# Five edits to a gated mix of block attention and a long convolution: where the convolution is added, how one table factor is summed, and a new order

## The chip, the cores and the metric

The kernel runs on one core of one Trainium2 chip. The metric is device time in microseconds of one execution. The engines are named as in the profile: PE (TensorE, the matrix engine; PEld are its weight loads), ACT (ScalarE), DVE (VectorE), POOL (GpSimd) and SP (SyncE, which issues nearly all DMAs here).

## The reference, cut to what matters

```python
x = A_x                                             # (1, 2048, 512) bf16
g = sigmoid((x * gate_w).sum(-1, keepdims=True))    # one gate per token
a = _A_ref(x, wq, wk, wv, wo, beta)                 # 32 heads of 16, 4 segments of 512 tokens
b = _B_ref(x, A_re, A_im, B_re, B_im, C_re, C_im, log_dt, Dskip)
return g * a + (1 - g) * b

# _A_ref, per segment s and head:
#   softmax attention inside the segment, plus a read of a running memory M, z
#   o = sigmoid(beta) * a_mem + (1 - sigmoid(beta)) * a_dot ;  a = concat(o) @ wo
# _B_ref, per channel d:
#   K[d, l] = Re sum_n C[d,n] * exp(dt*A[d,n] * l) * dt*B[d,n]     l = 0 .. 2047 (l rounded to bf16)
#   y = causal convolution of x[:, d] with K[d, :], by FFT ;  b = y + x * Dskip
```

## The kernel before, in words

The program is recorded as some 1,800 operations (class `Sched`). Each has an engine, a function that issues its instructions, and the buffers it reads and writes. The list `ORDER` gives the order of all of them by number, with the buffer slots and, for operations that may run on either engine, whether ACT or DVE takes them. `replay` walks that list; `emit` adds the semaphores. So each engine works through its own queue in a fixed order, and nothing is reordered at run time.

The work falls into these parts, which the order interleaves:

- **Attention.** For each of 4 segments and 4 groups of 8 heads, `project` makes q and k, `scores` makes five score groups. Each group is a matmul in four row tiles into one block of four PSUM banks (banks 0 to 3, the only one for scores), read by one exponential on ACT (L1063, 128x2048, 80 in all). Masks, sums with the values (17 columns a matmul) and normalization follow on PE and DVE. `ophase` reads the memory and transposes the result into `oTT`.
- **Tables.** For each of 4 blocks of 128 channels, `tables` builds powers of exp(dt*A) as two factors, F (20 exponents) and G (32 exponents, multiples of 8). `cmul` makes n new columns of a factor with three DVE products or sums (L1159, L1162, L1166). Then the sums over n of C, B and the powers ("lag") are made on PE: per slice of 4 state rows, four matmuls of 128x64 weights (slices of G) on 40 columns (slices of F), in two column tiles of 64 at `tile_position=(0, 64 * A)`. F and G have one buffer each, so the next block's table begins after these sums.
- **Convolution.** `x_level1` does the first level of a two-level transform of x and parks it in `scr_Z`. `tail` does the rest for two halves of the channels: 16 steps each of x's second level (tag X), K's transform from the tables (tag K), their product on DVE (tag Y), the inverse second level (tag V) and then the inverse first level (tag fir), whose result goes to `scr_C` and is reloaded by token into `CTT`.
- **Output.** `final(s, tb)`, 16 tiles of 128 tokens: on PE, 512 columns of the convolution through the identity, four matmuls of 128 columns that add the skip (x times a diagonal `diagT`), and four of 512 that multiply `oTT` by `wo`; then one scaled read of PSUM on ACT or DVE (L229, L230), and a store.

The gates: `gate_tokens` computes e^z for each token; attention is scaled by e^z (through `oms` and `einvT`) and the final read multiplies everything by 1/(1 + e^z), made for all tokens in `gate_final`.

The token-wise transpose of x comes from PE for segment 0 and from one transposing DMA of 512 KB per segment for the others (L717, issued by SP). All DMAs are issued by SP. The code was recorded with one helper for matmuls, so nearly all PE rows of the profile carry the line of that helper, L683; transposes have lines of their own (L732, L747, L938).

Of the kernel before, what the change touches and what calls it, by code (L numbers as in the profile page):

```python
# [8 lines left out]
BF16 = mybir.dt.bfloat16  # L9
# [339 lines left out]
def c_pe(mode, *ns):  # L349
    return ("P", mode, ns)  # L350
# [16 lines left out]
8/2 22/0 190/0 191 192 194/0 206/1 195 9/4 14/0 0/0 11/1 30/0 10/0 55/1 24/3/1 25v 31/3 26/6/2 6/0 58/2 39/10 40/12 56/4  # L367
1225/0 1243/0/0 1231/3/1 1233/5 27a 1/0 34/13 32/4 33/9 17/0 35 36 37 46/11 15/0 1241/1 38/5 174/0 41/4 179/7 12/0 59v/0
45/13 13/4 47/0 49/1 23/0 57a 201/2/1/1 48 19/0 42 60/3 1244a 62/2 43 44 51/6 61 63v/4 72/2 75v/5 74/6 21/0 73 50/4 54/0
64 202a 84/2 1234a 86/1 18 16 85 87v/2 76 193/0 203 99v/6 52/13 96/2 204/0/0 1242a 589/0 98/2 378/0 97 100 53 28/4/0  # L370
211/7 29a 175/2 108/3 109/1 65 101 205a 294/5/0/2 110 176/0 122/5 77 123v/3 295a 209/1 111v/0 3/0 1232a 180/0 197/4
251/2/2/0 1246/1 213/3 215/0/0/1 120/2 121 88 252a 256/2/1/0 177/1 210a 1245/0 89 212a 1235 182/2 590/1 198/0 178 135v/8
257 591 220/0/1 800/0 221 132/1 66/3 134/6 136 199/0 990v/0 253 258 214v 67/2 133 207/1 222 989v 144/3 137 68 254/2/1
216 112 113 259 208v 2/0 218 145/1 146 5/0 993v/0 159v/7 158/3 997 992v 241/0/3 255a 998/0 242 160 991v 200/0 999
1257/2/1 994 243 1259/1 1260a 80/0 1258a 229/0/2 230 124 78/1 338/1/2 156/3 1247/2/0 1249/3 231 995/1 157 224/0/0 1003
225 339a 379/1 217 161 1261 996 1007/0 1004/1 147v/9 1005 79 219/0/0 380 1000 1248a 223/1 1001/1 1006 125 801/2 1250a
148 1226/3/1 1002 802 226 168v/1 1010/1 237/0/1 238 90/1 1009 91/5 227 1228/2 1008 1227a 239 1251 228 297/3/0 298a 382/0
1011 169 272/0/0 592 170 273 92 296 1262/3/0 1012 232 233/1 1229a 1230 149 236/2 240 244 245 1015 274 1263a 234 263/0/2
264 246/0 260 1013/1 247 102/1 1264/3 235/1 265 1016/0 104/6 1265a 248 103 114/1 267/0/1 268 1266 381 266/1 1014 261/0
1252/2/1 1017 1254/3 1021 269 1236/0/0 115/7 280/0/2 281 1255a 270 271 1238/3 275 1018 1253a 282 116 1019/0 126/1 1020  # L380
1024 276/4 277 1237a 1028/1 1027 249/2 250a/0 278/1 1267/1 1029 284/0/3 285 286 335/0/1/0 593 1025/0 803 987/0 336a
308/0/1 1256 309 279/0 1026 1239a 283 287 1283/1/1 1031/1 1285/2 310 1030 4/0 1286a 288 289/2 304/0/3 1284a 1022/0 305
384/1/2/1 290 1032 340/2/1/1 306 385a 1023 321/0/2 322 1287 341 1037/1/0 1041/3 1038 128/1 1039 1042 127 342 1033/2 323
140/3 1034 1035 313/0/0 1040a 1043a 343 291 314 183 307/1 311 312 386 1050v/0 1036a 315 1052v/0 1049v 1288/0 1048v 1056
196 1057/1 1051v 1275/2/1 1058 117v/4 337 138/1 1240 1062 1046/0 69v/6 1063/1 1273/3 1274a 1276a 325/0/3 326 327 316
1054/0 1289/2/0 317/0 1053 1064 387/3/0 388a 1055 347/0/1 318 1069/1 348 395/0/0 1059 1290a 319/0 1065 299/1/0/0 1066/0
139 349 1067 1074 320/2 324 1277 1045 328 1075/0 300 1291/3 356/0/2 70 129v/5 1292a 329 302 152/4 330/1 331 392 357 396a
1299/0/1 1301/3 81v/7 358 130 1068 1076 301 105v/0 1300a 150/3 1302a 332 351/0/3 352 399/0 292/3 444/1/1 353 93v/3 82
1293 445a 368/0/0 151 1060/0 1077 369 1280/1/0 1070 350/2 354 400a 355 1303 293a 359 1268/0/1 131 370 1278/3 1281a 1279a
106 364/0/1 165v/2 1078/1 1079 365 366 1061 1071 1269a 1270/3 1271a 71 1086 393/1 83 406/0/3 407 1282 1087/0 363/0 367  # L390
1044 166 1088 1272 408 360/3 448/0 361 1072/1 362/1 1296/2/0 394a 333/3 1073 94 334a 95 371 372 373/4 410/0/0 167 411
1047 1080 1090/0 1297a 1294/1 1089 153v/8 397/2 141v/1 374 412 423/0/2 1091 375 154 424 1081/0 1304/3/1 398a 303/0 344
1295a 107 409/1 1306/2 118 1083 425 1298 427/0/3 428 1307a 1305a 1308 164/5 413 1322/0 1084/1 376/2 441/3/1/0 429 345
442a 415/0/1 1085 119 1082 155 416 1100/3/0 1101 1092/0 1093 377a 1094 1309/1 262 443 1096/2 1097 1098 414 391/1 142
162/2 163 383/0 181 417 346 171v/9 1107v/0 1099a 1310/0 1311/2 473/0/0 474 1111v/0 1110v 1113/0 1109v 1108v 1115 422/2
426 418 1116/1 1095a 1102a 1112 419/0 1114 1324/0 1117 542/3/2 420 430 431 1323/1 475 1105 1104 543a 1325/0/2 1326a 1118
# [129 lines left out]
def build_graph(nc, es, A_x, A_wq, A_wk, A_wv, A_wo, A_beta, B_A_re, B_A_im, B_B_re, B_B_im,  # L526
# [12 lines left out]
    def cload(arr, name, dt, key=0.0):  # L539
# [6 lines left out]
        S.dma(lambda: ap(T, n=n), lambda: h[:], 128 * n * sz, w=[T], key=key, q=LQ)  # L546
        return T
# [876 lines left out]
```

## Time and profile before

| | |
|---|---|
| Runs | 314.17, 313.51, 311.81 us; median 313.51 |
| Profiled execution | span 311.6 us from its first to its last instruction; its own time is not given apart from that |
| Granted PE clock, mean | 0.965 |
| First exponential | starts at 26.89 us |
| Last exponential | starts at 283.80 us |
| Last read of an output tile | starts at 305.20 us |
| DMA | 49.94 MB, mean 160 GB/s |

The page gives the busy time of each engine as a share of the span, and the same in 40 slices of 7.8 us, one digit of tenths each. Windows give the same for a chosen stretch. The chain of waits goes back from the last instruction, at each step to what released it. Rows of a timeline give start and duration in microseconds, then engine, line, operation, output and input, shape and count; matmuls that follow each other are merged into one row under the shape of the first. Since matmuls are pipelined, the start of one and the start of the next tell more than their durations.

### The profile page before, as it was taken

Reading aid. Unit: us, or ns where it says so; the run is one execution under the profiler, and the core shown is the slowest. Engines: PE = TensorE matmul, PEld = TensorE weight load, DVE = VectorE, ACT = ScalarE, POOL = GpSimd, SP = SyncE. Lnnn points to the kernel's source line nnn. Section 1 sums busy time; section 2 is a strip of 40 time slices with the busy share of each in tenths; the row PEclk is TensorE's granted clock in tenths of the full one; section 3 lists DMA queues with packets and bytes.
Section 4 is the critical chain, followed back from the end, with each engine's and each line's share of the span. In section 5 each row is a group of like instructions: output and inputs, shape, how many; then the busy total and the mean of one; then the engine's idle time right before and its main releaser. Section 6 shows DMA issues by size and latency. Waiting matters only on the chain.

```text
span 311.6 us, 9347 instructions
## 1 busy us (share of the span) xinstructions
PE 267.4 (86%) x3868; PEld 175.6 (56%) x3868; DVE 262.9 (84%) x638; ACT 270.0 (87%) x323; POOL 3.2 (1%) x9
## 2 busy tenths in 40 slices
PE   1787687698778899899988999999999999879991
PEld 1442354364444666586765576767767667555550
DVE  1999899989999989998999998989994999883440
ACT  2898998999999999989999989999899999985221
POOL 2000000000000000000000000000000000000000
PEclk9997995989998999999999999999999999998999
DMA  5999423151333754656665578787688784466141
GB/s 138 237 230 207 106 87 107 40 143 41 95 91 88 202 142 116 176 166 181 176 189 152 172 202 253 218 238 209 197 251 240 209 253 113 131 177 201 50 135 52
DMA packets 62362, 49.94 MB, mean 160 GB/s; under 512 B 23920, under 2 KB 57712, under 8 KB 62320
## 3 DMA queue, kind: packets, MB, share of 16 engines
q1 hardware_dynamic: 62320, 49.35, 56.7%
q8 instruction: 30, 0.49, 0.7%
q14 instruction: 12, 0.10, 0.1%
HBM read 29.02 MB, written 8.39 MB: 120 GB/s over the span
## 4 chain that ended last, share of the span: by engine, by line
PE 41%; ACT 35%; DVE 9%; DMA 7%; issue 4%; SPq 3%; DVEq 0%; ACTq 0%
PE psum L683 40%; ACT sb L1063 20%; ACT sb L226 12%; SPq L222 3%; DMA sb<-sb 2%; DVE sb L227 1%; DMA sb<-scr_Z 1%; DMA scr_C<-sb 1%; ACT sb L799 1%; DMA sb<-c_ident 1%; ACT sb L941 1%; DVE sb L1271 1%; ACT sb L992 1%; DMA sb<-c_negm 1%; DVE sb L1162 1%
## 5 line engine op out<-in xcount | busy, mean ns | idle before, releaser
L683 PE MATMUL psum<-sb 128*128 128x17 bf16 (+11 forms) x3780 | 261.2, 235 | 30.2 <-ACT sb L1063 17.6
L683 PEld LDWEIGHTS psum<-sb 128*128 128x128 bf16 (+3 forms) x3780 | 168.8, 99 | 119.3 <-ACT sb L1063 33.9
L1063 ACT ACTIVATE sb<-psum 128x2048 bf16<-128x2048 f32 x80 | 152.1, 1901 | 6.6 <-PE psum L683 6.4
L226 ACT ACTIVATE sb<-psum 128x512 bf16<-128x512 f32 (+3 forms) x171 | 100.3, 647 | 7.2 <-PE psum L683 6.4
L227 DVE CAST sb<-psum 128x512 bf16<-128x512 f32 (+1 forms) x52 | 35.3, 692 | 11.7 <-PE psum L683 10.0
L1159 DVE TENSOR_TENSOR sb<-sb 128x512 bf16<-128x512 bf16 (+3 forms) x52 | 34.0, 659 | 0.1
L1166 DVE TENSOR_TENSOR sb<-sb 128x512 bf16<-128x512 bf16 (+3 forms) x52 | 33.8, 661 | 0.1
L1162 DVE TENSOR_TENSOR sb<-sb 128x512 bf16<-128x512 bf16 (+3 forms) x52 | 33.7, 659 | 0.1
L1271 DVE TENSOR_TENSOR sb<-sb 128x1024 bf16<-128x1024 bf16 x32 | 21.8, 682 | 2.4 <-ACT sb L226 1.3
L1075 DVE TENSOR_TENSOR sb<-sb 128x1024 bf16<-128x1024 bf16 (+1 forms) x40 | 22.7, 576 | 1.0 <-ACT sb L1063 0.9
L229 ACT ACTIVATE sb<-psum,sb 128x512 bf16<-128x512 f32 x8 | 5.4, 686 | 14.9 <-PE psum L683 14.9
L1038 DVE TENSOR_TENSOR sb<-psum,sb 128x256 bf16<-128x256 f32 x32 | 13.3, 418 | 0.3
L230 DVE TENSOR_SCALAR sb<-psum,sb 128x512 bf16<-128x512 f32 x8 | 5.9, 747 | 6.9 <-PE psum L683 6.9
L1035 DVE RECIPROCAL sb<-psum 128x16 f32<-128x16 f32 x32 | 8.0, 251 | 4.2 <-PE psum L683 4.2
L799 ACT ACTIVATE sb<-sb 128x512 f32<-128x512 f32 x18 | 11.3, 643 | 0.0
L1115 DVE TENSOR_TENSOR sb<-psum,sb 128x512 bf16<-128x512 f32 x12 | 8.3, 688 | 0.2
L800 DVE TENSOR_TENSOR sb<-sb 128x256 f32<-128x256 f32 x18 | 7.5, 419 | 1.1 <-ACT sb L799 1.1
L747 PE MATMUL psum<-sb 128*128 128x128 bf16 x24 | 2.7, 280 | 6.4 <-DMA sb<-c_ident 6.3
L808 DVE CAST sb<-sb 128x512 bf16<-128x512 f32 x20 | 8.2, 420 | 0.0
L992 ACT ACTIVATE sb<-sb 128x512 bf16<-128x512 bf16 x12 | 7.6, 631 | 0.0
L801 DVE SCALAR_TENSOR_TENSOR sb<-sb 128x256 f32<-128x256 f32 x18 | 7.5, 419 | 0.0
L941 ACT ACTIVATE sb<-psum 128x512 bf16<-128x512 bf16 x12 | 7.3, 609 | 0.2 <-PE psum L938 0.2
(61 smaller groups left out, 92.4 us busy)
## 6 DMA issues: line engine op xcount, KB each, us to landing
sb<-c_DNM SPq DMA_DIRECT2D x32, 320.0 KB, 3.8
sb<-c_DNM SPq DMA_DIRECT2D x32, 192.0 KB, 3.0
sb<-sb SPq DMA_DIRECT2D x84, 64.0 KB, 2.9
scr_Z<-sb SPq DMA_DIRECT2D x16, 256.0 KB, 2.3
sb<-scr_Z SPq DMA_DIRECT2D x32, 128.0 KB, 3.3
sb<-sb SPq DMA_DIRECT2D x32, 128.0 KB
sb<-in_A_x_dram SPq DMA_DIRECT2D x5, 512.0 KB, 4.5
scr_C<-sb SPq DMA_DIRECT2D x8, 256.0 KB, 3.4
```

Of the source, the lines that this page charges most:

```text
L226: fa = lambda e: e.activation(dst(), src(), ACT.Copy)
L227: fd = lambda e: e.tensor_copy(dst(), src())
L683: mm = lambda e, o_, l, r_, st, sp, **kw: e.matmul(o_, lhsT=l, rhs=r_, start=st, stop=sp, skip_group_check=True, **kw)
L799: op("ACT", ("As", 512), lambda e, sq=sq, Z=Z: e.activation(ap(sq, n=512), ap(Z, n=512), ACT.Square), r=[Z], w=[sq], key=PW[h] + PWS * k)
L992: op("ACT", ("Asx", 512), lambda e: e.activation(ap(eq, n=512), ap(qT, n=512), ACT.Exp), r=[qT], w=[eq])
L1038: op("DVE", ("V1", 256), lambda e: e.tensor_tensor(ap(o1, gi * 16, [[128, 4], [32, 4], [1, 16]]), ap(T, dims=[[68, 4], [17, 4], [1, 16]]), ...
L1063: o = op("ACT", ("Ax", 2048), lambda e, P=P, pT=pT: e.activation(ap(pT, n=2048), ap(P, n=2048), ACT.Exp, scale=0.25), r=[P], w=[pT])
L1075: op("DVE", ("V2", 128 * nb), lambda e, pT=pT, dims=dims: e.tensor_tensor(ap(pT, dims=dims + [[1, 128]]), ap(pT, dims=dims + [[1, 128]]), ...
L1159: op("DVE", ("V2" if n > 1 else "V1", 256 * n), lambda e: e.tensor_tensor(run(tile, ne, dst, 1), run(tile, ne, src, sstep), ap(pw, cl * 51 ...
L1162: op("DVE", ("V2" if n > 1 else "V1", 256 * n), lambda e: e.tensor_tensor(run(t2, n, 0, 1), run(tile, ne, src, sstep), ap(pw, cl * 512 + 2 ...
L1166: op("DVE", ("V2" if n > 1 else "V1", 256 * n), lambda e: e.tensor_tensor(D_(), D_(), ap(t2, n * 128, [[-n * 128, 2], [2 * n, 64], [1, 2 * ...
L1271: op("DVE", ("V2", 1024), lambda e, Y=Y, XAB=XAB, K3=K3: e.tensor_tensor(ap(Y, dims=[[512, 2], [1, 512]]), ap(XAB, dims=[[512, 2], [1, 512 ...
```

## The change

1. **Final tiles.** The identity matmul and the skip leave PE. The sum in PSUM is now attention alone, scaled already by g = 1/(1 + e^-z), and DVE adds the convolution times (1 - g) while it reads PSUM, in one operation per tile (L1348). ACT no longer reads final tiles.
2. **Gates.** `gate_tokens` makes e^-z, 1 + e^-z, g and 1 - g per segment, `gate_final` is gone, and one exponential less is made for segments 1 to 3.
3. **Skip.** x times the diagonal is added in the inverse first level: four matmuls of 128 columns in each of 16 groups, with columns of x that are 16 tokens apart as weights.
4. **Table factor G.** Its upper 16 exponents are no longer completed as complex products. One DVE product makes the part that stays in place, two more make the second term, and the sums get the second term as extra matmuls: for each slice four of 128x32 weights, in column tiles of 32 at `(0, 64 * A + 32)`, on top of the four of 128x64.
5. **Loads.** The identity and the first block of x are issued by ACT; the rest by SP as before. Each transposing load is split in four.
6. **Order.** `ORDER` is new throughout. In it some operations change between ACT and DVE, the mask table is loaded earlier, exponentials and sines at the start stand in another order, and fewer of the final tiles stand behind the last exponential.

```diff
-ident = cload(np.eye(128), "ident", BF16, -1)
+ident = cload(np.eye(128), "ident", BF16, -1, q="ACT")
...
 def do_xT(s):
     if s > 0:
-        op("SP", ("D", 524288), lambda e: e.dma_start_transpose(
-            ap(xTT[0], s * 512, dims=[[2048, 4], [1, 512]]), ... [[512, 512], [1, 512]])),
-           w=[xTT[s]], isdma=True, tr=True)
+        for k in range(4):
+            op("SP", ("D", 131072), lambda e, k=k: e.dma_start_transpose(
+                ap(xTT[0], k * 2048 + s * 512, n=512), ... [[512, 512], [1, 128]])),
+               pw=[xTT[s]], isdma=True, tr=True)
...
 # gate_tokens
-    op("ACT", ..., activation(g(expT), g(gzT), ACT.Exp))
-    if s > 0:
-        op("ACT", ..., activation(g(einvT), g(gzT), ACT.Exp, scale=-1.0))
+    op("ACT", ..., activation(g(expT), g(gzT), ACT.Exp, scale=-1.0))
+    op("DVE", ..., tensor_scalar_add(g(einvT), g(expT), 1.0))
+    op("DVE", ..., reciprocal(g(gzT), g(einvT)))
+    op("DVE", ..., tensor_tensor(g(omgT), g(expT), g(gzT), ALU.mult))
...
 # tables
-        gm(16, 0, 1, 8, 7)
-        gm(24, 8, 1, 8, 7)
+        pw = pws[(7, h)]
+        rd = parts(gp, G, 0, 16)
+        op("DVE", ("V2", 4096), tensor_tensor(G[16:32], G[0:16], pw, ALU.mult))
+        tw = [Tile(t2P, BF16) for _ in range(2)]
+        for cc in range(2):
+            op("DVE", ("V2", 2048), tensor_tensor(tw[cc], G half cc [0:16], pw, ALU.mult))
...
                         for cc in range(2):
                             for A in range(2):
                                 pr = 32 * A + sl
                                 i = mm(e, ap(P, ..., p0=64 * A, np_=64), ap(G, (1 - cc) * GPL + pr * 2 * NG, n=2 * NG),
-                                       ap(F, ...), cc == 0, cc == 1, tile_position=(0, 64 * A))
+                                       ap(F, ...), cc == 0, False, tile_position=(0, 64 * A))
+                        for cc in range(2):
+                            for A in range(2):
+                                pr = 32 * A + sl
+                                i = mm(e, ap(P, ..., p0=64 * A + 32, np_=32), ap(tw[cc], pr * 32, n=32),
+                                       ap(F, ...), False, cc == 1, tile_position=(0, 64 * A + 32))
...
 # tail, inverse first level
+                    for j in range(2):
+                        for kk in range(2):
+                            k = 2 * half + kk
+                            i = mm(e, ap(P, j * 256 + kk * 128, n=128), ap(xTT[0], k * 2048 + b0 + j, [[16, 128]]),
+                                   ap(diagT, k * 128, n=128), False, j == 1 and kk == 1)
...
 # final
-            mm(e, ap(P, n=512), ap(ident, n=128), ap(CTT[s], tb * 512, n=512), True, False)
-            for k in range(4):
-                i = mm(e, ap(P, k * 128, n=128), ap(xTT[0], k * 2048 + t0, n=128), ap(diagT, k * 128, n=128), False, False)
-            for hg in range(3 if s == 3 else 4):
+            for hg in range(nh):
                 i = att(e, hg, hg == 3)
...
-        S.evac(lambda: ap(ou, n=512), lambda: ap(P, n=512), 512, r=[P, omgT], w=[ou], scale=lambda: ap(omgT, 4 * s + tb, n=1))
+        op("DVE", ("V1", 512), lambda e: e.scalar_tensor_tensor(ap(ou, n=512), ap(CTT[s], tb * 512, n=512), ap(omgT, 4 * s + tb, n=1),
+                                                                ap(P, n=512), ALU.mult, ALU.add), ...)
```

Two places of the new order matter below. The first is PE's queue around the table sums of the first channel block (64x40 and 32x40 are the outputs of those sums, 128x17 the sums with the values, 128x256 and 128x2x128 a score group and its mask). Before:

```order
L683 MATMUL psum<-sb 128x512 x4
L938 MATMUL psum<-sb 128x128 x4
L683 MATMUL psum<-sb 128x512 x4
L683 MATMUL psum<-sb 128x128 x4
L683 MATMUL psum<-sb 64x40 x128
L683 MATMUL psum<-sb 128x256 x8
L683 MATMUL psum<-sb 128x2x128 x4
L683 MATMUL psum<-sb 128x17 x32
```

and now, where its twelfth slice ends and the thirteenth begins:

```order
L686 MATMUL psum<-sb 64x40 x4
L686 MATMUL psum<-sb 32x40 x4
L686 MATMUL psum<-sb 128x512 x4
L686 MATMUL psum<-sb 128x128 x4
L686 MATMUL psum<-sb 64x40 x4
L686 MATMUL psum<-sb 32x40 x4
```

One run of 128 equal matmuls became 32 pairs of rows, one for each slice, alternating between the two tile shapes, with a score group between the twelfth and the thirteenth; the sums of the second block are cut twice by score groups, those of the third and fourth once by convolution steps or sums with the values.

The second place is the end of PE's queue, the final tiles behind the last score groups. Before, near the last transpose of an attention result:

```order
L683 MATMUL psum<-sb 128x512 x4
L683 MATMUL psum<-sb 128x128 x8
L683 MATMUL psum<-sb 128x512
L683 MATMUL psum<-sb 128x128 x4
L683 MATMUL psum<-sb 128x512 x5
```

and now:

```order
L686 MATMUL psum<-sb 128x512 x4
L686 MATMUL psum<-sb 128x17 x16
L686 MATMUL psum<-sb 128x512 x8
L686 MATMUL psum<-sb 128x128 x8
L686 MATMUL psum<-sb 128x512 x32
```

The identity matmuls (one of each five) and the skip (128x128 x4) are gone from it; the 128x128 rows that are left are the last transpose of an attention result. On DVE the queue now ends with eleven combinations of L1348, where the 16 reads were shared before, eight on DVE (L230) and eight on ACT (L229).

More of the change, by code (lines that the diff above doesn't have):

```diff
@@ L452 @@
[L452 to L455 removed]
+209/0 9/0 8/1 0/0 24/4/0 14/0 1229/0 6/0 1235/0/0 55/1 30/0 1245/1/1 25v 31/0 39/1 40/2 1237/4 3/0 34/3 32/4 1246a
@@ L537, in const, with cload @@
         return nc.inline_tensor(np.ascontiguousarray(arr, dtype=np.float32), name=name)
-    def cload(arr, name, dt, key=0.0):
+    def cload(arr, name, dt, key=0.0, q=LQ):
         arr = np.asarray(arr, np.float32).reshape(128, -1)
@@ L572, in build_graph @@
     omgT = S.keep(64, F32)
+    omgP = [omgT.part() for _ in range(4)]
     gzT = S.keep(64, F32)
@@ L723, in do_xT @@
               lambda: bass.AP(x.tensor, x.offset + s * 4 * 128 * 512, [[512, 128], [128 * 512, 4], [1, 512]]),
-              524288, w=[xks], key=(-0.95 if s == 0 else S.key - 8))
+              524288, w=[xks], key=-0.95, q="ACT")
         S.tag = "xT%d" % s
```

224 lines of the change are left out of this document (117 added, 107 removed).

## The prediction

> **What bounds the kernel now.** I read the page first, then busy time by windows, then the chain that ended last, and last the single rows around the places that the change touches.
>
> ```profile
> PE 267.4 (86%) x3868; PEld 175.6 (56%) x3868; DVE 262.9 (84%) x638; ACT 270.0 (87%) x323; POOL 3.2 (1%) x9
> PE   1787687698778899899988999999999999879991
> DVE  1999899989999989998999998989994999883440
> ACT  2898998999999999989999989999899999985221
> PE 41%; ACT 35%; DVE 9%; DMA 7%; issue 4%; SPq 3%; DVEq 0%; ACTq 0%
> L1063 ACT ACTIVATE sb<-psum 128x2048 bf16<-128x2048 f32 x80 | 152.1, 1901 | 6.6 <-PE psum L683 6.4
> ```
>
> Three engines are near 86%, so the average says little; the windows say more (columns: stretch, length, then busy time and count for PE, PEld, DVE, ACT, POOL, then granted clock, DMA share, GB/s).
>
> ```profile
> 60.00:80.00 20.00, 16.34 (x320) 9.67 (x316) 18.43 (x55) 19.73 (x24) 0.00 (x0) 0.91 0.29 86
> 187.00:284.00 97.00, 92.42 (x1314) 65.55 (x1307) 81.61 (x190) 89.86 (x91) 0.00 (x0) 0.98 0.72 210
> 284.00:306.00 22.00, 21.16 (x191) 12.15 (x189) 8.58 (x17) 6.96 (x9) 0.00 (x0) 1.00 0.32 104
> ```
>
> From about 20 to 120 us ScalarE (the 80 exponentials of L1063) and VectorE set the pace, and PE has some idle time: 20.00 - 16.34 = 3.7 us in 20. From 187 us on PE is the fullest. After the last exponential PE works alone. All 80 exponentials use one block of four PSUM banks, so the next scores cannot be computed until the exponential before has read the block, and nothing behind a late score group on PE can be done early: whatever lengthens PE's in-order queue between two exponentials delays the next one, unless PE was idle there.
>
> **The change part by part.**
>
> (1) Table sums ("lag"). Before, one channel block's sums are 128 matmuls of 128x64 weights on 40 columns. Now each slice has, behind its four matmuls into 64-row column tiles, four into 32-row tiles.
>
> The order on PE (shown with the change) turns one run of 128 equal matmuls into 32 slices that go back and forth between two tile shapes: 64 changes of shape for each of the four blocks. What a change of shape costs can be read where the 64-wide run ends. The rows below are PE rows of narrow windows, in pairs: the last 64-wide pair in flight, and the first matmul of another shape behind it.
>
> ```profile
> 65.20:67.45 2.25, 2.25 (x134) 2.19 (x136) 1.89 (x6) 2.25 (x3) 0.00 (x0) 1.00 0.71 250
> 67.25 0.41 PE L683 MATMUL psum<-sb 128*64 128x40 bf16 x6
> 67.37 0.29 PE L683 MATMUL psum<-sb 16*128 16x256 bf16 x4
> 103.73 0.33 PE L683 MATMUL psum<-sb 128*64 128x40 bf16 x4
> 103.85 0.23 PE L683 MATMUL psum<-sb 128*128 128x17 bf16 x3
> 183.04 0.33 PE L683 MATMUL psum<-sb 128*64 128x40 bf16 x4
> 183.16 0.24 PE L683 MATMUL psum<-sb 128*128 128x17 bf16 x3
> ```
>
> Inside the run 128 matmuls start within about 2.0 us, 0.03 us for each pair. Across the end the step is 0.12 us in all three places, whether the next tile is 16 rows high or the whole array. A change of shape costs about 0.09 us. Going in costs as much or more: behind four full-array transposes (0.22 us without a change of shape) the first 64-wide matmul came 0.38 us after their start.
>
> ```profile
> 132.70 0.39 PE L938 MATMUL psum<-sb 128*128 128x128 bf16 x4
> 132.92 3.44 PE L683 MATMUL psum<-sb 128*128 128x136 bf16 x42
> 136.20 0.39 PE L938 MATMUL psum<-sb 128*128 128x128 bf16 x4
> 136.58 0.28 PE L683 MATMUL psum<-sb 128*64 128x40 bf16 x7
> ```
>
> A change from 64-wide to 32-wide does not occur before the change, so its price is bounded: 0 (only the tile moves) to 0.16 (0.38 - 0.22). I take 0.09, since every change of shape that the trace shows costs that or more. The Trainium skill, page "TensorEngine Tiling (Array Packing)", section Key Properties, says that changing the tiling mode, and not just the tile, drains TensorE, and lists 128x64 and 128x32 as different modes: by it the sum is the one worked out here, without it the first rival's.
>
> A slice is then two steps of 0.03 inside a shape and two of 0.12 across, 0.30 us; 32 slices are 9.6 us against 2.0, so +7.6 us of PE for each block, 30 us for four. How much of it is on the path:
>
> ```profile
> 136.59 2.76 PE psum L683 x132
> 181.47 4.74 PE psum L683 x139
> ```
>
> In the chain of waits blocks 2 and 3 stand on PE itself, so their 7.6 us count in full: 15.2. Blocks 0 and 1 run while ScalarE leads. They are spread over two or three intervals of about 3 us, in each of which PE has 3.7 / 20 x 3 = 0.55 us idle, so 6.5 us each would be late; but VectorE, which is busy 18.43 of 20 there, works off what it has meanwhile, and I take half, 6.5 for both. Sum +21.7; bounds +15.2 and +28.2. Late next are the score groups behind the sums, and with them the exponentials and masks; also the next block's table, which overwrites the same F and G.
>
> (2) Table products on VectorE.
>
> ```profile
> L1162 DVE TENSOR_TENSOR sb<-sb 128x2048 bf16<-128x2048 bf16 x12 | 14.5, 1210 | 0.0
> L1166 DVE TENSOR_TENSOR sb<-sb 128x1024 bf16<-128x1024 bf16 x12 | 8.2, 680 | 0.1
> L230 DVE TENSOR_SCALAR sb<-psum,sb 128x512 bf16<-128x512 f32 x8 | 5.9, 747 | 6.9 <-PE psum L683 6.9
> L227 DVE CAST sb<-psum 128x512 bf16<-128x512 f32 x51 | 34.7, 693 | 11.7 <-PE psum L683 10.0 <-DMA scr_C<-sb 1.1
> ```
>
> A block loses six products of 2048 elements (6 x 1.21 = 7.3 us) and gets one of 4096 and two of 2048. From 1024 to 2048 costs 0.53, so 4096 is about 1.21 + 2 x 0.53 = 2.27; 4.7 in all. Four blocks save 10.3 us. Against that stand about 2 us of small gate operations and nine more PSUM reads that the new order gives VectorE (9 x 0.69 = 6.2), which ScalarE loses. Net, VectorE -2 and ScalarE -5.4 before the end.
>
> (3) Start.
>
> ```profile
> 2.80 3.48 DMA sb<-c_ident
> 10.88 1.28 ACT L776 ACT_TABLE_LOAD   x1
> 12.18 0.42 ACT L776 ACTIVATE sb<-sb 128x256 f32<-128x256 f32 x1
> ```
>
> The identity is issued first on ScalarE's queue instead of fifth on SP's, so about 2 us earlier. But the new order alternates exponentials and sines: five table loads instead of three, 2 x 1.30 (10.88 to 12.18) = +2.6 us on ScalarE. The Trainium skill, page "ScalarE: Activation LUTs", section What ACT_TABLE_LOAD costs, gives 2.66 us with a drain for each; by it the sum would be 2.7 us higher, but the rows show 1.30. Parts 2 and 3 together: -2, bounds 0 and -5.
>
> (4) Skip in the inverse sums: 16 groups get four matmuls of 128 columns, 0.22 us a group (132.70 to 132.92 above), 3.5 us in the stretch where PE is busy 92.42 of 97. Their weights are columns of x 16 elements apart; if such loads ran at half speed, 6. Four final tiles instead of three stand ahead of the last exponential, but shorter: -0.5. I take +3, bounds 0 and +6.
>
> (5) The end. A final tile loses the identity matmul and the four skip matmuls; VectorE alone (L1348) adds the convolution.
>
> ```profile
> 283.80 1.88 ACT L1063 ACTIVATE sb<-psum 128x2048 bf16<-128x2048 f32 x1 [1.78 <-PE psum L683]
> 303.89 0.69 ACT L229 ACTIVATE sb<-psum,sb 128x512 bf16<-128x512 f32 x1 [1.93 <-PE psum L683]
> 305.20 0.69 ACT L229 ACTIVATE sb<-psum,sb 128x512 bf16<-128x512 f32 x1 [0.62 <-PE psum L683]
> ```
>
> A tile took 305.20 - 303.89 = 1.31 us of PE for 3072 columns; 2048 take 0.87. Behind the last exponential PE has ten tiles, 8.7, and VectorE 12 of the 16 combinations at 0.75 (L230) = 9.0, behind 1.9 for the exponential and an estimated 2.4 for a mask of 1024 elements (0.68, as in the L1166 row) and two normalizations. VectorE ends later: the last read starts 12.6 us after 283.80 instead of 21.4, -9 (bounds -6, if the convolution's reloads land late, and -9.8, at the 0.69 of L227).
>
> **Sum** against the profiled execution's span of 311.6: 311.6 + 21.7 - 2 + 3 - 9 = 325.3. The three runs lie 0.2 to 2.5 us above that span, their median 1.9: **327 us**.
>
> **The rivals.**
>
> *Changing between 64 and 32 columns is free*, because only the column group moves. For it: no row shows that very change. Against: each change of shape that is shown costs 0.09 or more. A block's sums take 32 x 4 x 0.03 = 3.9 us, +1.9; blocks 0 and 1 hide it in PE's 3.7 us of idle time per 20, blocks 2 and 3 pay 3.8: 311.6 + 3.8 - 2 + 3 - 9 = 307.4, a time of **309**, faster.
>
> *The cost is there and mostly covered*: PE catches up behind each run, blocks 0 and 1 cost nothing and 2 and 3 half, +7.6. For it: PE idle time up to 120 us. Against: single-buffered scores. 311.6 + 7.6 - 2 + 3 - 9 = 311.2, **313**, no change.
>
> *SP's queue clogs*: twelve transposing loads in place of three.
>
> ```profile
> L717 SPq DMA_TRANSPOSE sb<-in_A_x_dram x3: 2072/3579/5981, 13.2 to 27.1; - x3
> ```
>
> If the issue time goes by instruction, it is 12 x 3.58 = 43 us instead of 11.6, and power copies and stores of level-one sums wait behind them; half of the 31 us on the path gives **343**. Against: each now moves a quarter, and they are spread out; if it goes by bytes it changes nothing, which I take.
>
> **How the numbers follow.** Forecast 0.66, free change 0.19, covered 0.09, clogged queue 0.06. The forecast's own range is 316 to 338, from its bounds without all extremes at once. The range given, 306 to 338, takes in the covered case and most of the free one. A measurement of this kernel tells about 1% from no change. Faster by over 1%: 0.19 x 0.7 + 0.09 x 0.2 + 0.66 x 0.04 = 0.18; within 1%: 0.66 x 0.05 + 0.19 x 0.2 + 0.09 x 0.6 = 0.12; slower: 0.70.
>
> **What would show it.** Right: the 64-wide and 32-wide matmuls of a block span near 9.6 us, ScalarE idles several microseconds for PE in each of the four places, and the last exponential starts near 306 while the last output read follows within 13 us. Wrong: a block's matmuls in about 4 us (free change), exponentials that keep their 3 us beat through the sums (covered), or transposing issues that take SP over 30 us (clogged). If the end still takes over 18 us, part 5 is wrong.

## The result, and the profile after

| | before | after |
|---|---|---|
| Median of four runs | 313.2 us | 354.5 us |
| Ratio | | 1.131 (1.123 to 1.138) |
| Profiled execution: span | 311.6 us | 349.4 us |
| Granted PE clock, mean | 0.965 | 0.896 |
| First exponential starts | 26.89 us | 28.80 us |
| Last exponential starts | 283.80 us | 330.70 us |
| From there to the end of the span | 27.8 us | 18.7 us |

The changed kernel is slower by 41 us, not by the 14 us forecast, and outside the range. The profiled execution's own time is 351.2 us. A few executions run slower than the rest at a lower granted clock (the profiled one of e1 below is among them); the medians count them, the ratios leave them out.

The page of the kernel after (busy time, the slices of PE and of its granted clock, the chain by engine, and the group of the 80 exponentials with the idle time before them), and last the granted clock of the kernel before:

```profile
PE 307.9 (88%) x4364; PEld 208.0 (60%) x4364; DVE 267.4 (77%) x653; ACT 266.8 (76%) x305; POOL 3.2 (1%) x9
PE   1775787999888999999999989999899989988993
PEclk9999598957999658997599998589999999999999
PE 50%; ACT 25%; DMA 10%; SPq 5%; issue 4%; DVE 4%; DVEq 0%
L1063 ACT ACTIVATE sb<-psum 128x2048 bf16<-128x2048 f32 x80 | 150.7, 1884 | 19.2 <-PE psum L686 18.3
PEclk9997995989998999999999999999999999998999
```

VectorE and ScalarE did about as much as before (267 us each) in a span that is 38 us longer, so both idle more. The exponentials waited 18.3 us for PE instead of 6.4. PE's share of the chain of waits went from 41% to 50%, and its clock stands at 5 to 7 tenths in eight of the 40 slices, instead of in two. The chain of the kernel after names the places (start, length, work):

```profile
65.63 15.42 PE psum L686 x219
109.68 18.77 PE psum L686 x342
158.49 19.49 PE psum L686 x264
207.03 23.90 PE psum L686 x348
325.49 18.30 PE psum L686 x184
343.81 0.75 DVE sb L1348
```

The first four are the four blocks' table sums with what stands behind them on PE; before, only blocks 2 and 3 were there, with 2.8 and 4.7 us. The windows below hold the pieces of the sums and nothing else: five pieces before, nine after (the order cuts the sums up); two and four of them are shown, and the row that adds up all. Before:

```profile
65.23:67.37 2.14, 2.14 (x130) 2.10 (x129) 1.89 (x6) 2.14 (x3) 0.00 (x0) 1.00 0.73 260
136.58:138.72 2.14, 2.14 (x129) 2.11 (x129) 2.14 (x8) 2.00 (x5) 0.00 (x0) 1.00 0.64 188
...
sum 9.02, PE 8.73 PEld 8.53 DVE 8.17 ACT 8.47 POOL 0.00; mean PE 1.75 PEld 1.71 DVE 1.63 ACT 1.70 POOL 0.00
```

After:

```profile
70.78:78.91 8.13, 8.13 (x161) 6.24 (x161) 0.35 (x2) 2.96 (x3) 0.00 (x0) 0.50 0.01 2
...
158.49:167.62 9.13, 9.13 (x192) 7.05 (x193) 3.91 (x13) 2.73 (x6) 0.00 (x0) 0.63 0.29 92
...
211.99:220.83 8.84, 8.84 (x197) 6.86 (x193) 3.48 (x11) 3.32 (x4) 0.00 (x0) 0.70 0.36 115
222.87:226.12 3.25, 3.25 (x67) 2.49 (x65) 1.50 (x7) 1.68 (x1) 0.00 (x0) 0.50 0.18 40
sum 48.54, PE 48.53 PEld 37.51 DVE 16.74 ACT 19.18 POOL 0.00; mean PE 5.39 PEld 4.17 DVE 1.86 ACT 2.13 POOL 0.00
```

The sums grew from 9.0 to 48.5 us, by 39.5 us. In the first row VectorE worked 0.35 us of 8.13 and ScalarE 2.96; VectorE's next operation, at 79.03 us, had waited 7.90 us for PE. The last column but two is the granted clock: full before, between 0.50 and 0.70 in these four. Two windows inside one run, at full and at half clock, give the price of a slice (eight matmuls):

```profile
158.55:160.81 2.26, 2.26 (x59) 1.78 (x60) 2.26 (x9) 1.77 (x4) 0.00 (x0) 1.00 0.71 197
162.00:166.07 4.07, 4.07 (x84) 3.12 (x84) 0.47 (x2) 0.00 (x0) 0.00 (x0) 0.50 0.02 6
```

2.26 / 59 x 8 = 0.31 us at full clock, 4.07 / 84 x 8 = 0.39 at half. So the alternating run is slow at once, and then the clock falls while it lasts. It stays at half behind the sums too, for 2.7 to 9.0 us more in each of the four blocks.

The other terms of the prediction, in rows of after: the new products and the final read, the transposing loads, and the stretches behind the 48th and behind the last exponential.

```profile
L1194 DVE TENSOR_TENSOR sb<-sb 128x4096 bf16<-128x4096 bf16 x4 | 9.1, 2284 | 0.0
L1199 DVE TENSOR_TENSOR sb<-sb 128x2048 bf16<-128x2048 bf16 x8 | 9.7, 1219 | 0.1
L1348 DVE SCALAR_TENSOR_TENSOR sb<-sb,psum 128x512 bf16<-128x512 bf16 x16 | 11.0, 737 | 2.2 <-PE psum L686 2.2
L721 SPq DMA_TRANSPOSE sb<-in_A_x_dram x12: 1142/1245/1356, 9.7 to 81.4; - x12
229.00:330.70 101.70, 95.83 (x1387) 71.00 (x1388) 87.05 (x202) 89.35 (x86) 0.00 (x0) 1.00 0.69 199
330.70:349.40 18.70, 13.07 (x112) 6.57 (x110) 12.42 (x24) 2.48 (x2) 0.00 (x0) 0.98 0.47 148
```

The single operations cost what was forecast (2.28 for 2.27, 0.74 for 0.75). Twelve transposing issues take about 12 x 1.245 (the median) = 14.9 us instead of 11.6: SP's queue did not clog.

### The profile page after: what moved, and what is told of

Its sections match the earlier page's. It is cut to its first block, busy times and chain, and to the rows that moved or that the text cites. A ratio compares the mean times of both kernels' runs of the same rounds, so it can differ in the third digit from the quotient of the medians.

```text
span 349.4 us, 10315 instructions
## 1 busy us (share of the span) xinstructions
PE 307.9 (88%) x4364; PEld 208.0 (60%) x4364; DVE 267.4 (77%) x653; ACT 266.8 (76%) x305; POOL 3.2 (1%) x9
## 4 chain that ended last, share of the span: by engine, by line
PE 50%; ACT 25%; DMA 10%; SPq 5%; issue 4%; DVE 4%; DVEq 0%
PE psum L686 50%; ACT sb L1063 13%; ACT sb L226 7%; SPq L222 5%; DMA sb<-scr_Z 3%; DMA sb<-sb 3%; DMA sb<-c_DNM 2%; DMA sb<-c_W 2%; ACT sb L803 2%; DVE sb L227 1%; ACT L780 1%; DVE sb L1075 1%; ACT sb L992 0%; ACT L898 0%; ACT L875 0%
## 5 line engine op out<-in xcount | busy, mean ns | idle before, releaser
L686 PE MATMUL psum<-sb 128*128 128x17 bf16 (+12 forms) x4276 | 301.5, 237 | 29.6 <-ACT sb L1063 12.7
L686 PEld LDWEIGHTS psum<-sb 128*128 128x128 bf16 (+4 forms) x4276 | 200.4, 103 | 127.0 <-issue 28.0
L1063 ACT ACTIVATE sb<-psum 128x2048 bf16<-128x2048 f32 x80 | 150.7, 1884 | 19.2 <-PE psum L686 18.3
L226 ACT ACTIVATE sb<-psum 128x512 bf16<-128x512 f32 (+1 forms) x162 | 95.0, 629 | 43.5 <-PE psum L686 42.2
L227 DVE CAST sb<-psum 128x512 bf16<-128x512 f32 (+2 forms) x60 | 40.9, 689 | 21.8 <-PE psum L686 19.9
L1159 DVE TENSOR_TENSOR sb<-sb 128x512 bf16<-128x512 bf16 (+3 forms) x44 | 24.4, 561 | 0.3
L1162 DVE TENSOR_TENSOR sb<-sb 128x512 bf16<-128x512 bf16 (+3 forms) x44 | 24.3, 555 | 0.2
L1166 DVE TENSOR_TENSOR sb<-sb 128x512 bf16<-128x512 bf16 (+3 forms) x44 | 24.2, 557 | 0.2
L227 DVE COPY sb<-sb 128x256 bf16<-128x256 bf16 x20 | 4.9, 293 | 22.6 <-PE psum L686 21.6
L1348 DVE SCALAR_TENSOR_TENSOR sb<-sb,psum 128x512 bf16<-128x512 bf16 x16 | 11.0, 737 | 2.2 <-PE psum L686 2.2
L1199 DVE TENSOR_TENSOR sb<-sb 128x2048 bf16<-128x2048 bf16 x8 | 9.7, 1219 | 0.1
L1194 DVE TENSOR_TENSOR sb<-sb 128x4096 bf16<-128x4096 bf16 x4 | 9.1, 2284 | 0.0
L227 DVE COPY sb<-psum 128x1024 bf16<-128x1024 bf16 x3 | 2.1, 685 | 7.3 <-PE psum L751 7.3
```

What stands on the lines that cost most here:

```text
L226: fa = lambda e: e.activation(dst(), src(), ACT.Copy)
L227: fd = lambda e: e.tensor_copy(dst(), src())
L686: mm = lambda e, o_, l, r_, st, sp, **kw: e.matmul(o_, lhsT=l, rhs=r_, start=st, stop=sp, skip_group_check=True, **kw)
L1063: o = op("ACT", ("Ax", 2048), lambda e, P=P, pT=pT: e.activation(ap(pT, n=2048), ap(P, n=2048), ACT.Exp, scale=0.25), r=[P], w=[pT])
L1159: op("DVE", ("V2" if n > 1 else "V1", 256 * n), lambda e: e.tensor_tensor(run(tile, ne, dst, 1), run(tile, ne, src, sstep), ap(pw, cl * 51 ...
L1162: op("DVE", ("V2" if n > 1 else "V1", 256 * n), lambda e: e.tensor_tensor(run(t2, n, 0, 1), run(tile, ne, src, sstep), ap(pw, cl * 512 + 2 ...
```

## The experiments

The theory that they test: the sums grew by their changes of shape, and all of that is on the path. Its rivals: (A) it is the number of matmuls; (B) it is the new order; (C) it is the granted clock. The table puts the runs together; "the sums" is the added length of the windows as above, and ratios are to the kernel before on the same chip.

| Run | matmuls per block | changes of shape per block | the sums, us | median, us | ratio (95%) |
|---|---|---|---|---|---|
| before | 128 | 0 | 9.0 | 313.2 | 1 |
| f1_no_second_term (new order) | 128 | 0 | 9.1 | 315.0 | 1.007 (1.003 to 1.011) |
| f2_second_64_wide (new order) | 256 | 0 | 21.6 | 322.7 | 1.031 (1.023 to 1.038) |
| e1_grouped (new order) | 256 | 16 | 25.5 | 325.4 | 1.041 (1.032 to 1.050) |
| e2_all32 (new order) | 384 | 0 | 30.0 | 337.2 | 1.079 (1.070 to 1.089) |
| after (new order) | 256 | 64 | 48.5 | 354.5 | 1.131 (1.123 to 1.138) |
| e3_before_alternating (old order) | 192 | 64 | 39.1 | 348.6 | 1.117 (1.109 to 1.126) |
| e4_before_256_equal (old order) | 256 | 0 | 24.0 | 332.5 | 1.065 (1.057 to 1.073) |

The rows that add up the windows of f1 and of f2:

```profile
sum 9.08, PE 8.88 PEld 8.71 DVE 8.48 ACT 8.93 POOL 0.00; mean PE 0.99 PEld 0.97 DVE 0.94 ACT 0.99 POOL 0.00
sum 21.61, PE 18.71 PEld 18.13 DVE 15.52 ACT 16.36 POOL 0.00; mean PE 2.08 PEld 2.01 DVE 1.72 ACT 1.82 POOL 0.00
```

### Without the second term, and with it in one shape (f1, f2)

```diff
 # f1: the matmuls of the second term go, VectorE's products stay
-                        for cc in range(2):
-                            for A in range(2):
-                                ... p0=64 * A + 32, np_=32), ap(tw[cc], pr * 32, n=32), ... (0, 64 * A + 32)
 # f2: they stay, as 64-wide ones on G
-... p0=64 * A + 32, np_=32), ap(tw[cc], pr * 32, n=32), ... tile_position=(0, 64 * A + 32))
+... p0=64 * A, np_=64), ap(G, (1 - cc) * GPL + pr * 2 * NG, n=2 * NG), ... tile_position=(0, 64 * A))
```

> The changed kernel with the 32-wide matmuls of the sums left out (the second term is still made by VectorE but not added, so G's upper half is incomplete): VectorE's work, the loads and the order stay, and the sums are 128 matmuls of one shape per block again. Theory (the 39 us by which the sums grew are all on the path): 349.4 - 39 = 310 us of span, 312 to 316 us. Rival (part of it only fills time in which the new order would wait anyway, for tables or loads): 320 to 335 us.

> The changed kernel with the second term's 32-wide matmuls replaced by 64-wide ones on G again (as many matmuls, 256 per block, all of one shape; the values added are not the second term). Theory: 128 matmuls more per block cost about 4 us each as in the old order, the changes of shape the remaining 5 to 6: 312 to 316 us plus 4 x 4 = 328 to 332 us, so the changes of shape alone are worth 22 to 26 us of the 354. Rival (small column tiles cost by themselves, changes little): 345 us or more, or under 320.

f1 came out at 315.0 us, inside the theory's 312 to 316: with order, loads and VectorE's work of the changed kernel, leaving out the 512 matmuls of 128x32 weights gives back (1.131 - 1.007) x 313 = 38.7 us. So the sums, and not the order, are the slowdown, and on balance next to nothing covered them. f2, at 322.7, was better than its 328 to 332: the second 128 matmuls of a block cost (1.031 - 1.007) x 313 = 7.5 us over four blocks, and the changes of shape with what they bring (1.131 - 1.031) x 313 = 31.3 us, 0.12 us for each of 256. The second 64-wide matmuls add to sums just written, as the 32-wide ones do, so that is not what costs. Of the 12.5 us by which f2's sums are longer than f1's, 8.3 reached the span (321.2 against 312.9): in one shape, a part was covered.

### The alternation alone, and the number alone, in the kernel before (e3, e4)

```diff
 # e3: the second pair of each slice as four 32-wide matmuls, the same sum
-                                i = mm(... p0=64 * A, np_=64), ap(G, (1 - cc) * GPL ..., n=2 * NG), ... cc == 0, cc == 1, tile_position=(0, 64 * A))
+                            i = mm(... p0=64 * A, np_=64), ap(G, GPL + ..., n=2 * NG), ... True, False, tile_position=(0, 64 * A))
+                                i = mm(... p0=64 * A + 32 * u, np_=32), ap(G, ... + 32 * u, n=32), ... tile_position=(0, 64 * A + 32 * u))
 # e4: each 64-wide matmul as two of 20 columns
+                        for u in range(2):
+                            ... ap(P, (sl - q0) * 2 * NF + NF * u, n=NF, ...), ..., ap(F, ... + NF * u, n=NF), ...
```

> The kernel before, with the second pair of each slice's 64-wide matmuls replaced by four 32-wide ones (the same sums): 192 matmuls per block instead of 128 and 64 changes of shape, nothing else touched, order as before. Theory: 32 slices of 2 x 0.03 + 0.03 + 2 x 0.11, about 0.3 us each, 10 us per block instead of 2.0 and all four on the path: 313 + 4 x 8 to 9 = 345 to 350 us. Rival A (number of matmuls): 1 us per block more, 313 to 317 us. Rival B (the new order is what costs): 313 to 317 us.

> The kernel before, with each 64-wide matmul of the sums split into two of 20 columns: 256 matmuls per block instead of 128, as many as the changed kernel has, all 64-wide. Theory: 4 us per block instead of 2, in full at two blocks and partly at the others: 317 to 321 us, the clock as before. Rival A (the number of matmuls is what costs): 10 us per block, 345 to 352 us.

e3 (348.6 us) lies in the theory's 345 to 350: nothing but the alternation turns the kernel before into one nearly as slow as the changed one. That refutes rivals A and B a second time. Its sums grew by 30.1 us and its span by 35.1 (346.7 against 311.6). The clock stays at half for 4.1 to 6.3 us behind each block's sums, outside these windows; that the other 5 us come from there is likely, but no run separates them. Its first block (the window of its sums):

```profile
64.54:74.48 9.94, 9.94 (x194) 7.37 (x193) 1.89 (x6) 3.02 (x4) 0.00 (x0) 0.63 0.19 66
```

e4 missed: 332.5 instead of 317 to 321. All matmuls are of one shape, and yet the sums take 24.0 us, not 4 x 256 x 0.016 = 16.4; they grew by 15.0 us, its span by 17.3. The timeline of PE in the second block shows why:

```profile
105.79 3.99 PE L683 MATMUL psum<-sb 128*128 128x256 bf16 x223
112.09 1.89 PE L683 MATMUL psum<-sb 128*64 128x20 bf16 x43 [2.31 <-issue]
```

PE runs 223 matmuls in a row (the row carries the shape of its first) and then stands still for 2.3 us, with "issue" as the cause: it waits for nothing that the profile shows. The same gap is in f2 and e2 (first row f2, then two of e2), in these two blocks too some 210 small matmuls from the start of the sums; elsewhere in e2 it comes after 120 to 270:

```profile
147.73 1.39 PE L686 MATMUL psum<-sb 128*64 128x40 bf16 x49 [1.89 <-issue]
152.02 1.98 PE L686 MATMUL psum<-sb 128*32 128x40 bf16 x215 [0.30 <-DVE sb L1199]
156.78 1.06 PE L686 MATMUL psum<-sb 128*32 128x40 bf16 x74 [2.78 <-issue]
```

The page lists the transfers of instructions by queue; here before, then e4:

```profile
q8 instruction: 30, 0.49, 0.7%
q8 instruction: 34, 0.56, 0.7%
```

Each is 0.49 MB / 30 = 16 KB. e4 has 1,024 small matmuls instead of 512, with a weight load each, and four such transfers more, one for 128 matmuls and their loads. At 0.016 us a matmul PE uses one up in 2.0 us. In all twelve gaps of over 0.5 us in e4, f2 and e2, one such transfer lands 1.2 to 1.5 us before PE goes on; and the alternating runs (e3 and the changed kernel), which use matmuls up more slowly, have no such gap. That the gap is PE waiting for the next transfer is the likely reading, but argued: no run changed these transfers.

### Fewer changes of shape (e1), another single shape (e2)

```diff
 # e1: 16 64-wide matmuls of four slices, then the 16 32-wide ones
-... cc == 0, False, tile_position=(0, 64 * A))
+... sl == sl0 and cc == 0, False, tile_position=(0, 64 * A))
+                    for sl in range(sl0, sl0 + 4):
                         for cc in range(2):
                             ... p0=64 * A + 32, np_=32), ap(tw[cc], pr * 32, n=32), ...
 # e2: each 64-wide matmul as two 32-wide ones
+                            for u in range(2):
+                                ... p0=64 * A + 32 * u, np_=32), ap(G, ... + 32 * u, n=32), ... tile_position=(0, 64 * A + 32 * u))
```

> The changed kernel, with the sums of each four slices regrouped: their sixteen 64-wide matmuls first, then their sixteen 32-wide ones. Same matmuls, same order of everything else, 16 changes of shape per block instead of 64. Theory (each change of shape holds PE about 0.1 us, and all of it is on the path): 256 matmuls 4 us + 16 x 0.09 = 5.4 us per block instead of 12, so four times 6.6 us less: 328 us. Rival A (the second term costs by its number of matmuls): no change, 354 us. Rival B (the new order costs): 354 us. Rival C (it is the granted clock, which falls to half whenever small tiles run with other work): the clock stays at half in the four stretches and the time over 345 us.

> The changed kernel, with each 64-wide matmul of the sums replaced by two 32-wide ones: 384 matmuls per block instead of 256, all of one shape, so no change of shape inside a slice. Theory: 384 x 0.0155 = 6.0 us per block instead of 12, four times 6 us less: 330 us. Rival A (cost by number of matmuls): half as many again, so 8 us more per block at worst: 360 to 385 us. Rival B (order): 354 or a little more. Rival C (clock): over 345 us at half clock.

e1, the same work with 16 changes per block instead of 64, came to 325.4 us (forecast 328): (1.131 - 1.041) x 313 = 28 us for a reordering of matmuls inside an operation. e2 has half as many matmuls again as the changed kernel, but one shape, and is 16 us faster than it by the ratios; it is 7 us over its forecast, again with gaps at "issue" (the row above: 2.78 us). Rival C is half right. e2 has no change of shape inside its sums, and still runs a piece of them at half clock, behind such a gap:

```profile
209.18:210.77 1.59, 1.38 (x99) 1.21 (x97) 1.42 (x7) 1.59 (x1) 0.00 (x0) 0.50 0.18 41
```

So the clock does not fall for changes of shape only. The two kernels with 64 changes per block are the slowest of the table by 11 us; below them the number of changes does not order the runs (e2 with none is slower than e1 with 16), since the length of the sums and the gaps count too.

### Edit 4 undone (e8)

```diff
-        (the product of 4096 and the two of 2048; the matmuls of the second term)
+        gm(16, 0, 1, 8, 7)
+        gm(24, 8, 1, 8, 7)
```

> The changed kernel with edit 4 alone undone: G's upper half completed by the two old products of three operations each, at the place of the new ones in VectorE's queue, and the sums again 128 matmuls of one shape per block. Theory (the lengthened sums are all on the path; the traces give 48 us of them now against 9 before): 39 us less, given back in part by 2.6 us more of VectorE per block: 315 to 320 us. Rival B (the new order itself costs at the four places): over 340 us. What is left above or below 313 is what the other five edits come to.

332.6 us, so neither forecast: 22 us less than the changed kernel, not 35 to 39. The group of its sums, the piece in block 1 in PE's timeline, and the window of a piece in block 0:

```profile
L686 PE MATMUL psum<-sb 128*64 128x40 bf16 x512 | 15.4, 222 | 5.7 <-DVE sb L1166 5.7
108.16 1.80 PE L686 MATMUL psum<-sb 128*64 128x40 bf16 x52 [3.04 <-DVE sb L1166]
70.38:73.18 2.80, 2.33 (x82) 2.32 (x83) 2.55 (x8) 2.69 (x3) 0.00 (x0) 0.50 0.00 0
```

In this order the sums begin when VectorE has the table. The old products take longer (6 x 1.21 = 7.3 us against 4.7), PE waits 5.7 us for them in blocks 0 and 1, and the clock stands at half for the sums behind (2.33 / 82 = 0.028 us a matmul instead of 2.14 / 130 = 0.016). So edit 4 does bring something where it stands, and f1, which has its shorter products and none of its matmuls, is 17 us faster than e8. The same group takes 9.9 us in f1, so the wait and the slower sums are 5.7 + 15.4 - 9.9 = 11 of these; the other 6 are not accounted for. The clock of the whole span is 0.904 in e8 against 0.958 in f1, so PE is slower behind the sums as well; what that costs was not measured. The matmuls of edit 4 cost more than twice what its products bring.

### The other edits: in the old order (b1), without the skip (e7, e7b), the start (e6, e5)

b1 takes edits 1 to 3 into the kernel before and its old order:

```diff
 # final, gate_tokens and the inverse first level as in the change; tables, sums, loads and ORDER as before
+        op("DVE", ("V1", 512), lambda e: e.scalar_tensor_tensor(ap(ou, n=512), ap(CTT[s], ...), ap(omgT, ...), ap(P, n=512), ALU.mult, ALU.add), ...)
```

> The kernel before with edits 1 to 3 alone: convolution added while VectorE reads a final tile, gates per segment, skip in the inverse first level; old table products and sums, old loads, and the old order (three small gate operations of VectorE per segment stand just ahead of the one that needs them, three of the four diagonals beside each other). Theory (the end gives 9 us, the skip costs between 0 and 4 us of PE behind the 48th exponential, nothing else is touched): 304 to 308 us, the last exponential at 284 to 288 us and the end 18 to 20 us behind it. Rival (the end's gain hangs on the new order, which has more final tiles ahead of the last exponential): 311 to 314 us.

310.1 us, ratio 0.994 (0.991 to 0.997): 0.6% faster than the kernel before. The time lies between the theory's 304 to 308 and the rival's 311 to 314; by the ratio it is 0.994 x 313.2 = 311 us, the rival's. The windows behind the 48th and behind the last exponential, for b1 and then for f1 (the new order, with sums as before):

```profile
188.30:285.60 97.30, 92.84 (x1352) 68.90 (x1359) 82.11 (x191) 89.64 (x90) 0.00 (x0) 1.00 0.70 205
285.60:309.30 23.70, 15.14 (x114) 7.12 (x116) 13.66 (x25) 1.88 (x1) 0.00 (x0) 0.97 0.40 124
191.40:294.20 102.80, 97.38 (x1387) 71.09 (x1387) 87.29 (x202) 89.37 (x86) 0.00 (x0) 0.98 0.68 197
294.20:312.90 18.70, 13.10 (x112) 6.58 (x111) 12.44 (x24) 2.47 (x2) 0.00 (x0) 0.94 0.47 150
```

Edits 1 to 3 alone shorten the end from 27.8 to 23.7 us and lengthen the stretch ahead of it by 0.9 (96.4 to 97.3). The new order takes another 5.0 us off the end but puts 5.5 us into the stretch, where PE has 97.4 us of work instead of 92.8. The rest of the end's gain was moved, not made. In all, f1 is (1.007 - 0.994) x 313 = 4 us slower than b1: even without the second term's matmuls, the shorter products, the loads and the new order together lose against edits 1 to 3 alone.

e7 leaves the skip's matmuls out, e7b reads their weights from neighbouring columns:

```diff
 # e7
-                            i = mm(e, ap(P, j * 256 + kk * 128, n=128), ap(xTT[0], k * 2048 + b0 + j, [[16, 128]]), ap(diagT, k * 128, n=128), ...)
 # e7b
-... ap(xTT[0], k * 2048 + b0 + j, [[16, 128]]) ...
+... ap(xTT[0], k * 2048 + 128 * (b0 + j), n=128) ...
```

> The changed kernel without the skip: the 64 matmuls of 128 columns in the inverse first level are left out, so the output lacks x times the diagonal. Theory (they are on PE's path behind the 48th exponential, 16 groups of about 0.26 us): the stretch from the 49th to the last exponential shrinks by 4 us (101.7 to about 97.5), time 350 us. Rival (the 5 us there come from the new order): the stretch stays at 101 us, 354 us.

> The changed kernel with the skip's weights read from 128 neighbouring columns of x instead of columns 16 apart (another token order, so the skip is wrong; all else the same). If the strided weights are what makes these matmuls start 62 to 72 ns apart instead of 55: 64 x 0.012 = 0.8 us less, 353.5 us. If strided weights load at half speed and PE waits for it: 2 to 3 us less.

355.5 and 353.3 us, against 354.5: no difference that these intervals (1.126 to 1.142 and 1.122 to 1.137) can tell. The stretch did not shrink without the skip, 102.9 us in e7 against 101.7, though PE had less to do (its clock was 0.97 there against 1.00, but in the third part of the stretch, at 1.00 in both, e7 is the longer one too, 35.0 against 33.7 us):

```profile
232.60:335.50 102.90, 94.31 (x1312) 66.56 (x1322) 86.86 (x202) 89.06 (x87) 0.00 (x0) 0.97 0.68 196
```

So the skip is not what lengthened it. e6 moves one exponential ahead of the sines, e5 gives the two first loads back to SP:

```diff
 # e6, ORDER
-... 37 46/7 45/8 47/9 41/10 ... 57a/0 190/0 48 44 ...
+... 37 46/7 190/0 45/8 47/9 41/10 ... 57a/0 48 44 ...
 # e5
-    ident = cload(np.eye(128), "ident", BF16, -1, q="ACT")
+    ident = cload(np.eye(128), "ident", BF16, -1)
-              524288, w=[xks], key=-0.95, q="ACT")
+              524288, w=[xks], key=-0.95)
```

> The changed kernel with one ScalarE operation moved: the exponential for the beta gate stands ahead of the first sine instead of between two sines, so that three table loads are left of five. Theory (ScalarE's queue sets the first exponential): 2 x 1.30 us earlier, first exponential at 26.2 instead of 28.8 us, time 351.5 us. Rival (something else sets the start, PE's transposes or the late loads): first exponential stays at 28 to 29, time 354 us.

> The changed kernel with the identity and the first block of x issued by SP again, at the same places of the order. If the two loads on ScalarE's queue are worth something: first exponential 1 to 2 us later (30 to 31), 355 to 356 us. If the start is set by other loads: first exponential 28 to 29 us, 354 us. If they are what makes it later than before: first exponential near 27, 352 us.

```profile
28.48 1.87 ACT L1063 ACTIVATE sb<-psum 128x2048 bf16<-128x2048 f32 x1
29.31 1.87 ACT L1063 ACTIVATE sb<-psum 128x2048 bf16<-128x2048 f32 x1
```

The first exponential of e6, then of e5; 28.80 in the changed kernel. Neither start tells anything by itself: the other traces in the new order whose start is the same code begin between 28.52 (f1) and 29.68 us (e7). What moves them most is when ScalarE has the load of log_dt. Here is the operation that reads it, before, in the changed kernel and in e6:

```profile
6.13 0.63 ACT L755 ACTIVATE sb<-sb 128x512 bf16<-128x512 bf16 x1 [2.01 <-DMA sb<-in_B_log_dt_dram]
7.40 0.63 ACT L759 ACTIVATE sb<-sb 128x512 bf16<-128x512 bf16 x1 [4.34 <-DMA sb<-in_B_log_dt_dram]
8.17 0.63 ACT L759 ACTIVATE sb<-sb 128x512 bf16<-128x512 bf16 x1 [5.13 <-DMA sb<-in_B_log_dt_dram]
```

From there to the first exponential ScalarE takes 20.8 us before, 21.4 in the changed kernel, 20.3 in e6 and 21.5 in e5. So two table loads fewer are worth about 1.1 us of 2.6 there, hidden in e6 by a load that landed 0.8 us later, and of the loads on ScalarE's queue no gain can be told. e6's time, 351.4 us (interval 1.116 to 1.132), is not told apart from the change either. e5's 359.1 us (1.142 to 1.157) is not explained: of the 5.2 us by which its trace is longer, 3.3 come behind the 48th exponential, and why is open. b1, with the old loads in the old order, starts its first exponential at 26.83, and its operation on log_dt at 6.18. So of the 1.9 us that the start is late, 1.3 are the later landing of log_dt and 0.6 ScalarE's own work; e3, in the old order as well, starts at 28.25, with log_dt at 7.80, so part of this varies from run to run.

## Why the prediction was wrong, step by step

**Direction and place were right, the size was not.** The span is 349.4 against the sum's 325.3, 24.1 us more. f1 divides that: of 349.4 - 311.6 = 37.8, the second term in the sums is 349.4 - 312.9 = 36.5, and all the rest 1.3. So 14.8 us of the error are term 1 (36.5 against 21.7) and 9.3 the other terms (+1.3 against -2 + 3 - 9 = -8).

**Term 1, table sums: +21.7 forecast, +36.5 shown.** Two steps failed.

- *A slice of 0.30 us, 9.6 us per block.* Right at full clock (0.31), but the term took full clock for granted. The runs themselves bring it down, a slice then takes 0.39, and a block's sums took 48.5 / 4 = 12.1 us. The four together grew by 39.5 us instead of 30.4.
- *"Blocks 0 and 1 ... I take half".* Of 30.4 us the forecast hid 8.7; of 39.5 only 3.0 did not reach the span (on balance: the half clock behind the sums adds to it, what other engines cover takes away). The chain of after has blocks 0 and 1 beside 2 and 3. The idle time of PE that was to take them up is spread over 60 us, while the wait comes at one place, and the other engines had little to do meanwhile (VectorE 0.35 of 8.13 us, its next operation waiting for PE). That this is because there is one block of score banks, one F and one G is likely, but no run gave them a second buffer. The prediction had said of the single-buffered scores just that, and then taken half all the same.

That the change of shape costs, and goes by the rows at the ends of the old runs (0.09), held at full clock: (0.31 - 8 x 0.016) / 2 = 0.09. With the clock's part in it f2 puts it at 0.12, and e1 at 28.2 / 192 = 0.15, for 48 changes fewer in each block. The Trainium skill, page "TensorEngine Tiling (Array Packing)", section Key Properties, says that a change of tiling mode drains TensorE; these runs agree that the change costs, and give the price, but do not show that it is a drain.

**Terms 2 and 3, start and VectorE: -2 forecast.** In f1 the first exponential is 1.6 us late and the 48th 4.0 us (191.4 against 187.4). The table loads that were counted as +2.6 are worth about 1.1 (e6), and the identity that was to come 2 us earlier brought nothing that e5 can tell. The step that failed is to price the new order and the new loads at nothing: log_dt, which ScalarE waits for, lands later (its operation starts 0.9 us later in f1, 1.3 in the changed kernel), and f1 loses another 2.4 us between the first and the 48th exponential. Where these go is open. VectorE's busy time, forecast 2 us shorter before the end, came out 4.5 us longer in all (267.4 against 262.9); its reads of final tiles alone took 5.1 us more (11.0 against 5.9).

**Term 4, skip: +3 forecast, +6.4 in that stretch.** The cause is another one: b1 has the skip and pays 0.9, e7 drops it and gains nothing. The new order put 4.5 us more of PE's work there.

**Term 5, the end: -9 forecast, -9.1 shown**, and the last read starts 343.81 - 330.70 = 13.1 us behind the last exponential (forecast within 13). The number is in part luck. The forecast had VectorE end last, with 12 combinations behind the last exponential; 14 stand there, and the chain has PE, for 18.30 us, in front of the last read. And 4.1 us of the gain are the edit's (b1), 5.0 the order's, which were paid for ahead of it.

**The rivals.** *Free change*: refuted by f2 and e3. *Mostly covered*: refuted by f1; 36.5 of 39.5 us reached the span. *Clogged queue*: refuted, 14.9 us of issues. The range's upper end, 338, had no mechanism behind it that brings the clock down; that is the rival that was missing. The clock of the kernel before, shown above, is at half in one slice already.

## What to carry to other kernels

Group small matmuls by tile shape: the same sums with 16 changes of shape instead of 64 per block took 28 us off this kernel, and the second term's matmuls, which cost 38.7 us here, cost 7.5 in the shape of the first. Before a saving on one engine is paid for on another, ask what can run while the other is busy; here, with single buffers behind it, PE time counted almost in full even where PE had shown idle time before. A gain at the end of a kernel should be measured together with the stretch ahead of it, since an order can move work from one to the other.

## What the runs showed of the hardware that was not expected

- The granted clock falls to half during long runs of alternating tile shapes, while PE issues a matmul every 0.04 to 0.05 us: 1.00 from 158.55 to 160.81 us, 0.50 from 162.00 on. The Trainium skill, page "TensorE: Matmul & The Clock Gate", section What's actually happening, has the clock set by how busy PE has been, in windows of about 3.4 us. Here the profile has PE busy in the whole of both windows (2.26 of 2.26 us and 4.07 of 4.07), so the busy time that the profile shows, with its modelled ends, is not what the gate goes by. What it does go by, the runs do not show.
- Matmuls into two column tiles of 64 start 0.016 us apart with 40 columns (before: 2.14 / 130), and with 20 as well (e4, the window below: 1.63 / 101): fewer columns gain nothing. Into tiles of 32 columns, four in turn for most, they start 0.009 us apart (e2: 1.98 / 215).

```profile
196.02:197.65 1.63, 1.63 (x101) 1.60 (x97) 1.22 (x6) 1.63 (x3) 0.00 (x0) 1.00 0.53 129
```

- After 120 to 270 small matmuls of one shape from the start of a block's sums, PE stood still for 0.8 to 2.8 us at no visible wait ("issue"), in e2, e4 and f2.
